# The first block of a two-layer attention and Mish kernel: order of loads, folds and products, and the order of its first stage

## The chip, the cores and the metric

The kernel runs on one core of one Trainium2 chip. Its time is in device microseconds (us) for one execution. A profiled execution has a span, from its first to its last instruction, and a time of its own a little above it. Engines are named as in the profile: PE is TensorE's matmuls and PEld its weight loads, DVE is VectorE, ACT is ScalarE, POOL is GpSimd, and SP is SyncE, which here issues the loads and stores.

## The reference, cut to what matters

Two layers, each of two residual steps, on x of 2048 x 640 in float32:

```python
x = x + A(layernorm(x))      # 32 heads of 20
x = x + B(layernorm(x))      # 640 -> 1536 -> 640, Mish between
# A:
q, k, v = split(x @ wqkv)
pq, pk = q @ w_phi, k @ w_phi                       # per head, 20 x 20
phi = concat(softmax(p), softmax(-p))               # for pq and pk
kv, z = phi_k^T v, sum(phi_k)                       # over the 2048 rows
o = (phi_q kv) / (phi_q z + 1e-6);   return o @ wo
```

q and k are used only through `w_phi`, so the kernel multiplies `w_phi` into the query and key weights once, at the start of layer 0. That is the "fold".

## The kernel before, in words

**Precision.** Every large product is made of three: each operand is split into a high part (rounded by a copy on ACT) and a low part (the rest, subtracted on DVE or POOL), and TensorE adds high x high, high x low and low x high. A projection of one tile of 128 rows onto 640 columns is `project` (L329): two halves of 320 columns, five chunks of 128 inputs each, three products, so 30 matmuls at L344.

**Stages.** Rows come in 8 blocks of two tiles of 128. The first stage of a layer is `attend_first` (L387): queries, keys and values of all tiles, their features, and the sums kv and z. The second is `attend_second`, then comes `dense`. A tile's queries and keys go through `features` (L355), a generator that stops after each step: the copy out of PSUM on ACT; minimum, maximum and differences on DVE (POOL takes one difference of a query); the exponential on ACT; sum and reciprocal on DVE and a product on POOL. Each step of the loop calls `advance` (L399), which moves every pending generator one stop further. A key tile ends in 22 matmuls that add to kv and z (L414, 11 calls); a query tile ends in a transposition on DVE (L423) and four stores. `order` (L464 to L470) says which of k, q and v of which tile comes at which of the six steps of a block. For a middle block it is k0, v0, q0, k1, v1, q1.

**PSUM and buffers.** PSUM has two wide tiles `mm` (L66), for projections, and four narrow ones `one` (L69); kv and z keep two of the narrow ones from block 0 to the end of the stage. Five `big` tiles hold key features and, at the end of the stage, reloaded query features.

**What orders the work.** The program text gives each instruction a place, and a planner (`tc.block(schedule_with_timeline_sim=True)`, L814) orders each engine from it by its own estimate of when operands are ready. `tc.manual_schedule(engines=...)` takes an engine's order from the text instead. `tc.issue_after(ins)` puts an instruction behind another one of the same engine, and `act` (L110) chains most of ACT's work that way. In the first block only SP is written by hand (L446).

**The first block of layer 0** (L445 to L458). SP loads, in this order: the first half of the table `phi_bd` of folded heads, chunks 0 to 2 of the transposed query weights (`load_raw`, 120 rows each), x of block 0 (`fetch_normed`, L390), the second half of the table, chunks 3 to 5. Then come five loads of value weights and six chunks of key weights. x is normalized: statistics on DVE (L250), a power on POOL (L260), two ACT operations (L303), then five transpositions of each tile on TensorE (L280) with their splits (L285, L286). `fold_phi` (L227) multiplies the chunks by the table: for each of five output rows k and two halves c, three products at L237 (the last chunk has 40 rows), then the split at L242 and L243. A product at L237 is in full float32 and appears as two instructions. `load_v_weights` splits the value weights (L127, L128). Block 0 takes v0, q0, v1, k0, q1, k1, and the key fold, `fold_phi` again, is called before k0 (L480).

Of the kernel before, what the change touches and what calls it, by code (L numbers as in the profile page):

```python
# [1 line left out]

# [6 lines left out]
F32 = mybir.dt.float32  # L9
# [33 lines left out]
def kernel(  # L43
# [76 lines left out]
    def v_tile():  # L120
        return work.tile([P, VW], F32, tag="v", name="v", bufs=2)

    def split(hi, lo, src, stage):

        st = stage()[:, :D]
        nc.sync.dma_start(st, src)
        nc.scalar.activation(hi, st, AF.Copy)  # L127
        nc.vector.tensor_tensor(lo, st, hi.bitcast(F32), op=ALU.subtract)  # L128

    def r1_spare(tag):  # L130
# [36 lines left out]
    def load_v_weights():  # L167

        ws = [r1_pair(k) for k in range(KD)]
        for k in range(KD):  # L170
            split(ws[k][0][:, D:2 * D], ws[k][1][:, D:2 * D], wv[k * P:(k + 1) * P, :],
                  (row_tile, row_tile, v_tile, v_tile, big_tile)[k])
        return ws

    def load_q_weights():
# [48 lines left out]
            raw.append((r, rows))  # L224
        return raw

    def fold_phi(ws, bd, raw):  # L227

        pss = {}
        for k, c in ((0, 0), (1, 0), (2, 0), (3, 0), (0, 1), (1, 1), (2, 1), (3, 1), (4, 0), (4, 1)):  # L230
            if c == 0:
                mm = None if k % 2 else mm_tile()
                pss[k] = [one_tile(), one_tile()] if k % 2 else [mm[:, 0], mm[:, 1]]
            ps = pss[k][c]
            for t in range(3 * c, 3 * c + 3):
                r, rows = raw[t]
                nc.tensor.matmul(ps[:, (t % 3) * 120:(t % 3) * 120 + rows],  # L237
                                 r[:rows, k * P:(k + 1) * P], bd[:rows, t, :rows],
                                 start=True, stop=True)
            n0, n1 = (0, 360) if c == 0 else (360, D)  # L240
            hi, lo = ws[k][0][:, n0:n1], ws[k][1][:, n0:n1]
            nc.scalar.activation(hi, ps[:, :n1 - n0], AF.Copy)  # L242
            nc.vector.tensor_tensor(lo, ps[:, :n1 - n0], hi.bitcast(F32), op=ALU.subtract)  # L243


    def norm_stats(t, xt):
# [79 lines left out]
        return Transposed(cols=cols)  # L326


    def project(xts, t, ws, col, ps=None):  # L329
# [57 lines left out]
    def attend_first(layer, x_src, first):  # L387


        def fetch_normed(b):  # L390
            if layer:
                return load_turned(n2_d[b], [row_tile] * 3)
            xt = fetch(x_src, b)
# [12 lines left out]
        def keys(xts, i, v):  # L406
            e = big_tile()
            yield from features(project(xts, i % BT, kv_ws, 0), e, False)
            yield
            for g in range(G):  # L410
                p, n = divmod(g, 2)
                w, m = (120, 64) if g < 10 else (80, 42)
                acc, c = (kva, 120 * p) if p < 4 else (kvz, 120 * (p - 4))
                nc.tensor.matmul(acc[64 * n:64 * n + m, c:c + w], v[:, GW * g:GW * g + m],  # L414
                                 e[:, 120 * g:120 * g + w],
                                 start=(i == 0 and p in (0, 4)), stop=(i == NT - 1),
                                 skip_group_check=True)
# [12 lines left out]

        def values(xts, i, v):
            vv = v.rearrange("p (h d) -> p h d", d=DH + 1)
            act(vv[:, :, DH], ident[:, :H], AF.Copy, scale=0.0, bias=1.0)
            if i < BT:
                pv = project(xts, i, kv_ws, D, [one_tile(), one_tile()])
# [7 lines left out]
            yield  # L443

        if first is None:  # L445
# [12 lines left out]
            nc.sync.dma_start(mask, head_mask)  # L458
        else:
            nxt, kv_ws = first  # L460
            q_ws = load_q_weights()
        for b in range(NB):
            xts = nxt
            order = ("k0", "v0", "q0", "k1", "v1", "q1")  # L464
            if b == 0:
                order = ("v0", "q0", "v1", "k0", "q1", "k1")
            elif b == 1:
                order = ("k0", "q0", "k1", "v0", "q1", "v1")
            elif b == NB - 1:
                order = ("k0", "k1", "v0", "v1", "q0")  # L470
            vs = [v_tile() for _ in range(BT)]
            for n, (kind, t) in enumerate(order):
                t = int(t)
                i = b * BT + t
                if b == 0 and n == 1:
                    if layer:
                        load_k_weights(kv_ws)
                if b == 0 and n == 3:
                    if layer == 0:
                        fold_phi(kv_ws, bd, raw)  # L480
                    kva, kvz = one_tile(), one_tile()
                if b == NB - 1 and n == 3:
                    loaded = {0: load(0)}
                if b + 1 < NB:
                    if n == 0:
                        xt = fetch_normed(b + 1)
                    elif n == 2:
                        nxt = xt if layer else normed(b + 1, xt)
                    elif n > 2:
                        nxt.step()  # L490
                g = {"k": lambda: keys(xts, i, vs[t]), "q": lambda: queries(xts, i),
                     "v": lambda: values(xts, i, vs[t])}[kind]()
                next(g)
                advance()
                pending.append(g)
# [401 lines left out]
```

## Time and profile before

| | us |
|---|---|
| median of three runs | 1401.89 |
| lowest and highest | 1401.17, 1402.03 |
| the profiled execution | 1400.33 |
| its span | 1398.6 |
| TensorE busy (99%) | 1384.2 |
| VectorE busy (77%) | 1074.5 |
| ScalarE busy (42%) | 584.1 |
| GpSimd busy (32%) | 442.3 |

A line of the profile that names a group has the line of the program, the engine, the operation, the tiles (out<-in), shapes and count; then busy time and the mean length of one in ns; then the idle time of the engine just before these instructions and what ended it. A line in the order of time begins with its start and its length in us, and merges equal neighbours (x8). A line of stretches has the stretch, its length, the busy time and count of each engine, the granted clock of TensorE, the share of the DMA engines and GB/s. Matmuls overlap: one's length is its time in flight, and the distance between two starts is what it costs TensorE. So TensorE counts as busy also where it runs at half its pace.

### The profile page before, as it was taken

Reading aid. Unit: us, or ns where it says so; the run is one execution under the profiler, and the core shown is the slowest. Engines: PE = TensorE matmul, PEld = TensorE weight load, DVE = VectorE, ACT = ScalarE, POOL = GpSimd, SP = SyncE. Lnnn points to the kernel's source line nnn. Section 1 sums busy time; section 2 is a strip of 40 time slices with the busy share of each in tenths; the row PEclk is TensorE's granted clock in tenths of the full one; section 3 lists DMA queues with packets and bytes.
Section 4 is the critical chain, followed back from the end, with each engine's and each line's share of the span. In section 5 each row is a group of like instructions: output and inputs, shape, how many; then the busy total and the mean of one; then the engine's idle time right before and its main releaser. Section 6 shows DMA issues by size and latency. Waiting matters only on the chain. (4 is left out here: it accounts for less than half of the span.)

```text
span 1398.6 us, 28120 instructions
## 1 busy us (share of the span) xinstructions
PE 1384.2 (99%) x11528; PEld 1367.6 (98%) x11528; DVE 1074.5 (77%) x1820; ACT 584.1 (42%) x973; POOL 442.3 (32%) x334
## 2 busy tenths in 40 slices
PE   7999999999999999999999999999999999999998
PEld 7999999999999999999999999999999999999998
DVE  5798877696698877788769887887767876767775
ACT  4444344321355454545454333332234444444443
POOL 1354444343422222222234443433352211211112
PEclk9999999999999999999999999999999999999999
DMA  8533422689733423343374333357976212333200
GB/s 319 169 79 57 75 40 39 185 237 292 254 87 95 111 75 64 91 114 95 106 273 89 71 65 69 50 109 218 288 251 208 69 26 77 95 95 95 73 24 20
DMA packets 350035, 169.57 MB, mean 121 GB/s; under 512 B 286866, under 2 KB 323458, under 8 KB 349906
## 3 DMA queue, kind: packets, MB, share of 16 engines
q1 hardware_dynamic: 349906, 167.78, 44.2%
q8 instruction: 90, 1.47, 0.4%
q14 instruction: 39, 0.32, 0.1%
HBM read 104.82 MB, written 62.91 MB: 120 GB/s over the span
## 5 line engine op out<-in xcount | busy, mean ns | idle before, releaser
L735 PE MATMUL mm<-r2h,ol 128*128 128x320 f32 x1280 | 304.7, 309 | 0.0
L719 POOL TENSOR_TENSOR ol<-big,ol 128x512 fp32r<-128x512 f32 (+1 forms) x98 | 129.8, 1325 | 484.1 <-ACT ol L718 407.8
L693 PE MATMUL one<-xtl,r1h 128*128 128x256 f32 x960 | 268.2, 279 | 0.0
L693 PE MATMUL one<-xth,r1l 128*128 128x256 f32 x960 | 268.0, 279 | 0.0
L693 PE MATMUL one<-xth,r1h 128*128 128x256 f32 x960 | 265.9, 279 | 0.0
L735 PEld LDWEIGHTS mm<-r2h,ol 128*128 128x128 f32 x1280 | 219.1, 188 | 0.0
L735 PE MATMUL mm<-r2l,ol 128*128 128x320 f32 x640 | 197.3, 309 | 0.0
L344 PE MATMUL mm<-r1h,xth 128*128 128x320 f32 x600 | 188.3, 314 | 0.0
L344 PE MATMUL mm<-r1h,xtl 128*128 128x320 f32 x600 | 185.7, 310 | 0.7 <-DVE xtl L286 0.7
L344 PE MATMUL mm<-r1l,xth 128*128 128x320 f32 x600 | 185.6, 309 | 0.0
L693 PEld LDWEIGHTS one<-xtl,r1h 128*128 128x128 f32 x960 | 180.4, 188 | 0.0
L693 PEld LDWEIGHTS one<-xth,r1l 128*128 128x128 f32 x960 | 180.4, 188 | 0.0
L693 PEld LDWEIGHTS one<-xth,r1h 128*128 128x128 f32 x960 | 179.6, 188 | 0.0
L708 DVE TENSOR_SCALAR big<-big 128x512 f32<-128x512 f32 (+1 forms) x98 | 56.4, 575 | 110.7 <-ACT big L706 110.5
L379 POOL TENSOR_TENSOR r<-r,r 128x1280 f32<-128x1280 f32 x32 | 75.8, 2367 | 142.6 <-DVE r L378 136.8
L735 PEld LDWEIGHTS mm<-r2l,ol 128*128 128x128 f32 x640 | 120.2, 188 | 0.0
L710 ACT ACTIVATE big<-big,two 128x512 f32<-128x512 f32 (+1 forms) x98 | 70.1, 715 | 116.1 <-DVE big L709 116.1
L706 ACT ACTIVATE big<-one,b1s 128x256 f32<-128x256 f32 x192 | 80.8, 467 | 90.2 <-PE one L693 89.7
L718 ACT ACTIVATE ol<-big 128x512 fp32r<-128x512 f32 (+1 forms) x98 | 61.0, 622 | 135.8 <-DVE big L717 135.7
L344 PEld LDWEIGHTS mm<-r1h,xth 128*128 128x128 f32 x600 | 112.8, 188 | 2.0
L344 PEld LDWEIGHTS mm<-r1h,xtl 128*128 128x128 f32 x600 | 112.8, 188 | 1.1 <-DVE xtl L286 1.0
L344 PEld LDWEIGHTS mm<-r1l,xth 128*128 128x128 f32 x600 | 112.8, 188 | 0.0
(129 smaller groups left out, 3158.1 us busy)
## 6 DMA issues: line engine op xcount, KB each, us to landing
e_d<-r SPq DMA_DIRECT2D x128, 160.0 KB, 4.0
big<-e_d SPq DMA_DIRECT2D x32, 640.0 KB, 6.8
x_d<-xt SPq DMA_DIRECT2D x23, 640.0 KB, 4.1
xt<-x_d SPq DMA_DIRECT2D x22, 640.0 KB, 4.4
n_d<-xn SPq DMA_DIRECT2D x176, 80.0 KB, 2.1
xt<-in_x SPq DMA_DIRECT2D x16, 640.0 KB, 5.7
xn<-x_d SPq DMA_DIRECT2D x28, 320.0 KB, 4.6
v<-n_d SPq DMA_DIRECT2D x30, 256.0 KB, 2.9
```

The costliest lines, as they stand in the source:

```text
L344: nc.tensor.matmul(ps[:, :HC], a[:, sl], r, start=(k == 0 and n == 0), stop=(k == KD - 1 and n == 2))
L379: nc.gpsimd.tensor_tensor(eg, eg, r.unsqueeze(2).to_broadcast([P, 2 * H, DH]), op=ALU.mult)
L693: nc.tensor.matmul(ph[:, j, :], l, r, start=(n == 0), stop=(n == 3 * KD - 1))
L706: exps[0] = nc.scalar.activation(part(ta, 0)[:, j - js.start], ph[:, j, :], AF.Exp, bias=b1s[:, 2 * pr + j:2 * pr + j + 1]).ins
L708: nc.vector.tensor_scalar_min(e, e, E_CAP)
L710: nc.scalar.activation(r, n, AF.Ln, bias=two)
L718: nc.scalar.activation(ah[:, js], n, AF.Copy)
L719: nc.gpsimd.tensor_tensor(al[:, js], n, ah[:, js].bitcast(F32), op=ALU.subtract)
L735: nc.tensor.matmul(pys[t][:, c, :HC], l[:, j, sl], r, start=(f == 0 and n == 0), stop=(f == KF - 1 and n == 2))
```

## The change

1. **Warm transposes.** Before everything else TensorE transposes the identity 36 times into a narrow PSUM tile that nobody reads (`keep_warm`), and four times more between each two of the first three fold chunks.
2. **Loads.** x of block 0 is loaded first. The loads of x of block 1 and of the mask are issued behind the key chunks.
3. **Written order.** In the first block, and through all six steps of block 0 of layer 0, TensorE follows the text.
4. **Query fold by chunk.** The first halves of all five rows are folded chunk by chunk (five rows with chunk 0, then chunk 1, then 2), and split; then come the transposes of x; then the second halves, one piece between each two groups of three products of the first half of q0.
5. **Order of block 0.** q0 comes first: q0, v0, v1, k0, q1, k1. The value weights are split on ACT behind the last query piece. The ten key pieces stand one by one between the ten groups of three products of v1.
6. **By kinds.** Middle blocks (2 to 6, in both layers) take k0, k1, v0, v1, q0, q1, and a key of an even tile of blocks 2 to 6 gets one more stop ahead of its accumulation, which so comes in the same step as that of the odd tile.

The diff, cut to its core:

```diff
+    warm = one_tile()
+    def keep_warm(n):
+        for _ in range(n):
+            nc.tensor.transpose(warm[:, :P], ident, ident)
+    keep_warm(36)
...
-    def split(hi, lo, src, stage):
+    def split(hi, lo, src, stage, behind):
...
-        nc.scalar.activation(hi, st, AF.Copy)
+        with nullcontext() if behind is None else tc.issue_after(behind):
+            nc.scalar.activation(hi, st, AF.Copy)
...
+    def fold_heads(bd, raw, k, t, ps):
+        r, rows = raw[t]
+        nc.tensor.matmul(ps[:, (t % 3) * 120:(t % 3) * 120 + rows], r[:rows, k * P:(k + 1) * P],
+                         bd[:rows, t, :rows], start=True, stop=True)
+    def fold_split(ws, k, c, ps):
+        n0, n1 = (0, 360) if c == 0 else (360, D)
+        hi, lo = ws[k][0][:, n0:n1], ws[k][1][:, n0:n1]
+        ins = nc.scalar.activation(hi, ps[:, :n1 - n0], AF.Copy)
+        nc.vector.tensor_tensor(lo, ps[:, :n1 - n0], hi.bitcast(F32), op=ALU.subtract)
+        return ins.ins
+    def fold_part(ws, bd, raw, k, c, ps):
+        for t in range(3 * c, 3 * c + 3):
+            fold_heads(bd, raw, k, t, ps)
+        return fold_split(ws, k, c, ps)
...
         for c in range(2):
-            project_half(ps[c], xts, t, ws, col, c)
+            for ks in [range(KD)] if between is None else [range(k, k + 1) for k in range(KD)]:
+                project_half(ps[c], xts, t, ws, col, c, ks)
+                if between is not None:
+                    next(between, None)
...
             yield from features(project(xts, i % BT, kv_ws, 0), e, False)
             yield
+            if i % BT == 0 and BT < i < NT - BT:
+                yield
...
-            with tc.manual_schedule(engines={mybir.EngineType.SP}):
+            with tc.manual_schedule(engines={mybir.EngineType.PE, mybir.EngineType.SP}):
+                xt = fetch_normed(0)
                 bd = big_tile()[:120, :720].rearrange("p (t c) -> p t c", t=6)
                 nc.sync.dma_start(bd[:, :3], phi_bd[:, :3])
                 raw = load_raw(0, range(3))
-                xt = fetch_normed(0)
                 nc.sync.dma_start(bd[:, 3:], phi_bd[:, 3:])
                 raw += load_raw(0, range(3, 6))
-                nxt = normed(0, xt).all()
+                nxt = normed(0, xt)
                 q_ws = [r2_pair(k) for k in range(KD)]
-                fold_phi(q_ws, bd, raw)
-                kv_ws = load_v_weights()
+                ps = [h for mm in (mm_tile(), mm_tile()) for h in (mm[:, 0], mm[:, 1])] + [one_tile()]
+                for t in range(3):
+                    for k in range(KD):
+                        fold_heads(bd, raw, k, t, ps[k])
+                    keep_warm(4 if t < 2 else 0)
+                for k in range(KD):
+                    fold_split(q_ws, k, 0, ps[k])
+                nxt.all()
+                mm = mm_tile()
+                q0 = [mm[:, 0], mm[:, 1], mm]
+                project_half(q0[0], nxt, 0, q_ws, 0, 0, range(1))
+                for k in range(KD):
+                    folded = fold_part(q_ws, bd, raw, k, 1, one_tile())
+                    project_half(q0[0], nxt, 0, q_ws, 0, 0, range(k + 1, min(k + 2, KD)))
+                project_half(q0[1], nxt, 0, q_ws, 0, 1)
+                kv_ws = load_v_weights(folded)
                 raw = load_raw(1)
-            nc.sync.dma_start(mask, head_mask)
+                xt = fetch(x_src, 1)
+                nc.sync.dma_start(mask, head_mask)
+            def fold_keys():
+                for k in range(KD):
+                    mm = mm_tile()
+                    for c in range(2):
+                        fold_part(kv_ws, bd, raw, k, c, mm[:, c])
+                        yield
...
-            order = ("k0", "v0", "q0", "k1", "v1", "q1")
+            order = ("k0", "k1", "v0", "v1", "q0", "q1")
             if b == 0:
-                order = ("v0", "q0", "v1", "k0", "q1", "k1")
+                order = ("v0", "q0", "v1", "k0", "q1", "k1") if layer else ("q0", "v0", "v1", "k0", "q1", "k1")
...
+            with written(b == 0 and not layer):
...
-                    if layer == 0:
-                        fold_phi(kv_ws, bd, raw)
```

`written(on)` is `tc.manual_schedule` of TensorE, or nothing. `queries` of tile 0 gets the finished q0, and `values` of tile 1 gets `fold_keys()` as `between`.

More of the change, by code (lines that the diff above doesn't have):

```diff
@@ L1 @@
-from contextlib import ExitStack
+from contextlib import ExitStack, nullcontext
 import concourse.bass as bass
@@ L165, in r2_pair, with load_v_weights @@
         return tuple(wts.tile([P, D], F32R, tag=f"r2{s}{j}", name=f"r2{s}{j}") for s in "hl")
-    def load_v_weights():
+    def load_v_weights(behind=None):
         ws = [r1_pair(k) for k in range(KD)]
@@ L171, in load_v_weights @@
             split(ws[k][0][:, D:2 * D], ws[k][1][:, D:2 * D], wv[k * P:(k + 1) * P, :],
-                  (row_tile, row_tile, v_tile, v_tile, big_tile)[k])
+                  (row_tile, row_tile, v_tile, v_tile, big_tile)[k], behind)
         return ws
@@ L225, in load_raw @@
         return raw
[L227 to L243, printed above, removed]
+    def fold_heads(bd, raw, k, t, ps):
[12 more added lines that the diff above has]
+        return fold_split(ws, k, c, ps)
     def norm_stats(t, xt):
@@ L326, in load_turned, with project @@
         return Transposed(cols=cols)
-    def project(xts, t, ws, col, ps=None):
+    def project(xts, t, ws, col, ps=None, between=None):
         if ps is None:
@@ L387, in attend_first, with fetch_normed @@
     def attend_first(layer, x_src, first):
-        def fetch_normed(b):
+        def fetch_normed(b, xt=None):
             if layer:
                 return load_turned(n2_d[b], [row_tile] * 3)
-            xt = fetch(x_src, b)
+            xt = fetch(x_src, b) if xt is None else xt
             norm_scale(b, [norm_stats(t, xt) for t in range(BT)])
@@ L429, in queries, with values @@
                     yield
-        def values(xts, i, v):
+        def values(xts, i, v, between=None):
             vv = v.rearrange("p (h d) -> p h d", d=DH + 1)
@@ L434, in values @@
             if i < BT:
-                pv = project(xts, i, kv_ws, D, [one_tile(), one_tile()])
+                pv = project(xts, i, kv_ws, D, [one_tile(), one_tile()], between)
                 for c in range(2):
@@ L471, in attend_first @@
             vs = [v_tile() for _ in range(BT)]
[L472 to L478, printed above, removed]
-                    if layer == 0:
-                        fold_phi(kv_ws, bd, raw)
[L481 to L495, printed above, removed]
+            with written(b == 0 and not layer):
+                for n, (kind, t) in enumerate(order):
+                    t = int(t)
+                    i = b * BT + t
+                    if b == 0 and n == 1:
+                        if layer:
+                            load_k_weights(kv_ws)
+                    if b == 0 and n == 3:
+                        kva, kvz = one_tile(), one_tile()
+                    if b == NB - 1 and n == 3:
+                        loaded = {0: load(0)}
+                    if b + 1 < NB:
+                        if n == 0:
+                            xt = fetch_normed(b + 1, xt if b == 0 and not layer else None)
+                        elif n == 2:
+                            nxt = xt if layer else normed(b + 1, xt)
+                        elif n > 2:
+                            nxt.step()
+                    g = {"k": lambda: keys(xts, i, vs[t]), "q": lambda: queries(xts, i, q0 if first is None and i == 0 else None),
+                         "v": lambda: values(xts, i, vs[t], fold_keys() if first is None and i == 1 else None)}[kind]()
+                    next(g)
+                    advance()
+                    pending.append(g)
             if b == 1:
```

2 lines of the change are left out of this document (added).

## The prediction

> **What bounds the kernel now.** I read the page first, then the waits of TensorE, then the order of time around the first block and around one middle block, and last a few stretches.
>
> ```profile
> span 1398.6 us, 28120 instructions
> PE 1384.2 (99%) x11528; PEld 1367.6 (98%) x11528; DVE 1074.5 (77%) x1820; ACT 584.1 (42%) x973; POOL 442.3 (32%) x334
> PE   7999999999999999999999999999999999999998
> ```
>
> TensorE is full in every slice of 35 us but the first (and the tail of the last). So the change can win in the first 35 us, or by making TensorE's own work shorter. The waits of TensorE (who waited for what: us in total, times, longest) agree: the first fold (L237) waits 7.9 us for three loads, and the next entry is 0.9.
>
> ```profile
> PE mm L237 <- DMA raw<-in_wqk_t: 7.9, 3, 4.2
> PE mm L571 <- PE mm L571: 0.9, 2, 0.4
> ```
>
> A second loss hides inside "busy". In the order of time (start, length, engine, line, tiles, count):
>
> ```profile
> 0.99 0.29 POOL masks.py:199 TENSOR_SCALAR_AFFINE_SELECT ident<-ident 128x128 f32<-128x128 f32 x1
> 4.18 1.18 PE L237 MATMUL mm<-big,raw 120*128 120x120 f32 x4 [4.18 <-DMA raw<-in_wqk_t]
> ...
> 11.14 2.10 PE L237 MATMUL mm<-big,raw 120*128 120x120 f32 x8 [2.22 <-DMA raw<-in_wqk_t]
> 13.17 1.07 PE L237 MATMUL mm<-big,r 40*128 40x40 f32 x4
> 14.23 0.90 PE L280 MATMUL one<-ident,xn 128*128 128x128 f32 x3
> 14.93 1.48 PE L237 MATMUL one<-big,raw 120*128 120x120 f32 x6
> 16.20 1.70 PE L280 MATMUL one<-ident,xn 128*128 128x128 f32 x7
> 17.69 1.09 PE L237 MATMUL mm<-big,raw 120*128 120x120 f32 x6
> ...
> 45.61 0.60 PE L237 MATMUL mm<-big,raw 120*128 120x120 f32 x4
> 46.14 0.41 PE L237 MATMUL mm<-big,r 40*128 40x40 f32 x2
> 46.48 0.41 PE L344 MATMUL mm<-r1l,xth 128*128 128x320 f32 x1
> ```
>
> From 16.20 to 17.69 seven transposes start 0.213 us apart, and the six fold products before them 0.212. At 45.61 four fold products fit in 0.60 us; less one product's 0.27 in flight that is 0.11 apart. So TensorE is half as fast at first and doubles within the row of 17.69 (six products in 1.09), at about 18.3. It had worked without a pause since 11.14: that took 7.15 us.
>
> To compare the two kernels I take a point that both reach. The last fold piece of before ends at 46.48, and by then these instructions are done (stretch, its length, busy and count of TensorE, then of its weight loads; L237, L344 and L280 in turn):
>
> ```profile
> 0.00:46.47 46.47, 20.63 (x120) 18.83 (x120) 1.00 0.82 299
> 0.00:46.47 46.47, 16.40 (x103) 15.14 (x103) 1.00 0.82 299
> 0.00:46.47 46.47, 4.14 (x20) 3.07 (x20) 1.00 0.82 299
> ```
>
> All 120 fold instructions (a call at L237 is two of them), 103 projection matmuls, 20 transposes. I walk the changed block until TensorE has done as much.
>
> **The first block after the change.** Prices first: the splits on ACT and DVE (of fold pieces, of transposes, of value weights: count, busy, mean ns), two places where TensorE goes from folds to projections, and the way of x to its normalized rows.
>
> ```profile
> L242 ACT ACTIVATE r2h<-mm 128x360 fp32r<-128x360 f32 x3 | 1.4, 473 | 6.5 <-PE mm L237 6.5
> L116 ACT ACTIVATE xth<-one 128x512 fp32r<-128x512 f32 x3 | 1.8, 594 | 0.2 <-PE one L280 0.2
> L286 DVE TENSOR_TENSOR xtl<-one,xth 128x512 fp32r<-128x512 f32 x3 | 2.0, 683 | 0.2 <-ACT xth L116 0.2
> L127 ACT ACTIVATE r1h<-v 128x640 fp32r<-128x640 f32 x2 | 1.5, 737 | 0.0
> L128 DVE TENSOR_TENSOR r1l<-v,r1h 128x640 fp32r<-128x640 f32 x2 | 1.6, 814 | 0.0
> 25.80 0.42 PE L344 MATMUL one<-r1h,xth 128*128 128x320 f32 x1
> 26.05 0.31 PE L344 MATMUL one<-r1l,xth 128*128 128x320 f32 x1
> 43.02 0.83 PE L237 MATMUL mm<-big,raw 120*128 120x120 f32 x6
> 43.61 0.39 PE L344 MATMUL mm<-r1h,xth 128*128 128x320 f32 x1
> 9.92 1.66 DVE L250 BATCH_NORM_STATS2 bn<-xt 128x6 f32<-128x320 f32 x4
> 13.26 0.92 ACT L113 ACTIVATE xn<-xt,stats 128x640 f32<-128x640 f32 x1 [3.83 <-DVE stats L262]
> 15.00:20.00 5.00, 5.00 (x32) 5.00 (x31) 5.00 (x14) 5.00 (x11) 2.00 (x3) 1.00 1.04 401
> 803.21 13.40 PE mm L344 x90
> ```
>
> A second-half fold piece (4 + 2 instructions) takes 46.48 - 45.61 = 0.87; a first-half one (6) takes 43.61 - 43.02 = 0.59 behind transposes, and I take 0.65 between projections. The first projection matmul behind a piece holds TensorE 0.25 (25.80 to 26.05); in a long run one takes 13.40 / 90 = 0.149. So a group of three behind a piece takes 0.55.
>
> 1. Warm transposes. They need only the identity, ready at 0.99 + 0.29 = 1.28, so they start at 1.4. By the one example here TensorE doubles 7.15 later, at 8.55: 34 at 0.213, two at 0.11, end 8.85.
> 2. First halves of the query fold, chunk by chunk: 30 x 0.11 and twice four warm transposes, 8 x 0.11, together 4.2: end 13.05. Loads don't hold this: half table, three chunks and x are the first five loads in both kernels, and x, their last before, was in by 9.92. Now x is first; its way to two normalized rows (13.26 + 2 x 0.92 - 9.92 = 5.2) from about 5 on is over by 10.2, hidden. Ten transposes: 14.15.
> 3. The chunk order finishes five pieces nearly at once, so on ACT their high halves queue ahead of those of the transposes: first piece at 12.4, 5 x 0.47 = 14.75, then 0.59 and DVE's 0.68: 16.05. This wait is new; the first three products end at 16.2, 1.5 late.
> 4. Five second-half pieces (4.35) with four groups of three between (2.2), then 15 products (2.3): query tile 0 is done at 25.1.
> 5. Value weights are split behind the last query piece on ACT, from 23.2: 0.73, then on DVE 5 x 0.81, end 28.0. TensorE needs the last part at about 26.9, so value tile 0's first half ends at 28.15, the second 15 x 0.149 later: 30.4. Late by 1.1.
> 6. Value tile 1 with ten key pieces: 10 x 0.55 + 5 x 0.87 + 5 x 0.65 = 13.1, end 43.5. The switches (0.10 for each group behind a piece) are 1.0 of this and 0.5 of step 4. ACT and DVE need about half a us for a piece against 1.3 on TensorE, which hides them.
> 7. To the same point: 13 projections and ten transposes of the next block, 3.1. End **46.6**, against 46.48.
>
> So the front is worth **+0.1**: what it gains by starting early and without load waits is paid back by 8.85 us before the first useful product, 0.9 of inner warm transposes, 2.6 of waits for ACT and DVE, 1.5 of switches. Bounds: -1.7 to +3.1 by the moment of doubling, and up to +2.7 by DVE's order (rivals).
>
> Written order means that all of TensorE queues behind a late operand; steps 3 and 5 are such places. On the load queue mask, x of block 1 and the key chunks now come behind five value loads. The key chunks are needed first at about 31; the queue moves 401 GB/s (stretch from 15 to 20), 0.8 for a load of 327,680 bytes, and has them in by 21. I cost that at nothing; if the cover failed, each load late is 0.8.
>
> **The order by kinds.** In blocks 2 to 6 of both layers two keys come first, and the extra yield puts the even tile's accumulation (L414) beside the odd one's. Groups of 22 and of 44 and what follows them:
>
> ```profile
> 118.90 1.38 PE L414 MATMUL one<-big,v 128*64 128x120 f32 x22
> 120.21 0.42 PE L344 MATMUL mm<-r1h,xth 128*128 128x320 f32 x1
> 267.98 2.54 PE L414 MATMUL one<-big,v 128*64 128x120 f32 x44
> 270.45 0.41 PE L344 MATMUL one<-r2h,xth 128*128 128x320 f32 x1
> ```
>
> 22 take 1.31 and 44 take 2.47, so a merged pair saves 0.15, and up to 0.10 more where one slow re-entry into projections goes: I take 0.19, near the first. Ten blocks: **-1.9**. Bounds: 0 if they don't merge, -2.5 with all of it.
>
> **Sum.** 0.1 - 1.9 = -1.8. The profiled execution took 1400.33 (span 1398.6 and 1.7 around it), 1.56 under the median of the runs, 1401.89. The difference goes onto the median: **1400.1 us**.
>
> **Rivals.**
>
> (a) TensorE doubles sooner. The 7.15 us contain 1.06 of 40-row products (13.17 to 14.23) that may not count like full ones. If it doubles at 5.0, 17 transposes at 0.213 and 19 at 0.11 end at 7.1. The first chunk ends 1.16 MB of loads; 0.5 MB were in at 4.18 and 1.81 MB at 9.92, so about 7.1 too. Steps 2 to 7 come 1.75 earlier: 1398.4. [...]
>
> (b) Transposes alone don't raise the speed. Then 36 slow ones end at 9.07, the doubling comes 7.15 after the first product, at 16.2, and step 2 ends at 16.7, not 13.05. ACT keeps up with slow products, which gives back 0.6: +3.1, **1403.2**. For it: no row shows a doubling on transposes alone. Against it: from 14.23 to 17.69 transposes took 2.19 of 3.46, and the doubling came next. [...]
>
> (c) DVE is held by x of block 1. That load lies behind 20 others, 6.8 MB with its own: 1.81 by 9.92, then 0.4 a us, so about 22.5. If its statistics (1.66 and some 0.3) stand in DVE's order ahead of the second-half low parts, these end at 26.7 and the value parts at 30.7, not 28.0: +2.7, 1402.8. It decides only if the planner puts them there.
>
> (d) Slower. Keys and queries of neighbouring blocks now come four in a row, and DVE falls behind. Stretches of one middle block and of the last one (length, busy of PE, PEld, DVE, ACT, POOL):
>
> ```profile
> 118.90:149.37 30.47, 30.47 (x236) 29.85 (x235) 25.25 (x35) 12.16 (x17) 13.87 (x9) 1.00 0.37 66
> 240.00:268.00 28.00, 28.00 (x217) 27.19 (x215) 21.31 (x24) 9.18 (x12) 13.09 (x7) 1.00 0.56 118
> ```
>
> A block asks 25.25 of DVE in 30.47. Should all of it fall in four of six steps (20.3), DVE lags 4.9; without statistics and transposes (1.9 and 3 x 0.6), 1.2. ACT's next copy stands behind an exponential that waits for DVE, and with two PSUM tiles TensorE is held from a lag of one projection on, 30 x 0.149 = 4.5. At a lag of 5.2 each of ten blocks loses 0.7: +7, **1407**. Against it: the last block already runs keys, keys, values, values, query with TensorE full.
>
> (e) The change doesn't do all it says: from block 1 on the planner, not the text, orders TensorE. Groups kept apart cost the 1.9: 1402.0. It belongs to the forecast's own spread.
>
> **How the numbers follow.** Forecast with (e) 0.38 (own range 1398.3 to 1402.0), (a) 0.24, (b) 0.14, (c) 0.10, (d) 0.14. The range leaves out (d) and a little at both ends: **1396.5 to 1404.5**. A measurement of this kernel can tell about 0.2%, 2.8 us: faster is under 1399.1, slower over 1404.7. Faster: 0.18 of (a), 0.14 of the forecast, 0.02 of others, 0.34. Slower: 0.13 of (d), 0.04 of (b) and (c), 0.17. Same: 0.49.
>
> **What will show it.** Transposes from 1.4 on, 0.213 apart and then 0.11: where that changes decides between forecast, (a) and (b). TensorE waiting at 14 to 16 for the halves of the transposes, and in value tile 0 for L128's parts. Groups of 44 at L414 in blocks 2 to 6 in 2.47, no new wait at L344 or L414. The forecast is wrong if the work counted above (120, 103, 20) is done far from 46.6, or if what follows it is shorter by other than 1.9.

## The result and the profile after

The changed kernel takes 1410.25 us (median of 6 runs, 1408.29 to 1413.59), the kernel before 1401.53 in the same session (1400.68 to 1402.90): a ratio of 1.0065, interval 1.0053 to 1.0077. It is slower by 0.65%, and its time lies outside the range of the prediction. The profiled execution took 1408.29, the fastest of the six; its span is 1406.5. Lines below are those of the changed kernel (in the runs whose edits add lines, the same groups stand up to two lines further on); fold products are now L239, their splits L245 (ACT) and L246 (DVE), projections L356, transposes L289, warm transposes L92, key accumulation L428, value splits L136 (ACT) and L137 (DVE), statistics L259.

The page first, which hardly tells the two apart:

```profile
span 1406.5 us, 28222 instructions
PE 1387.9 (99%) x11572; PEld 1370.8 (97%) x11572; DVE 1073.5 (76%) x1820; ACT 584.6 (42%) x973; POOL 440.5 (31%) x334
PE   8899999999999999999999999999999999999998
```

TensorE is "busy" 3.7 us more for 44 more instructions, and the second slice of 35 us now shows an 8. The waits of TensorE say where (who waited for what: us in total, times, longest):

```profile
PE mm L239 <- DVE r1l L246: 6.2, 5, 2.3
PE mm L356 <- DVE r2l L246: 1.7, 1, 1.7
...
PE mm L356 <- DMA v<-in_wv: 1.3, 1, 1.3
PE one L356 <- DVE r1l L137: 1.0, 2, 0.8
```

The load waits of before are gone; five waits of fold products for DVE stand in their place. In the order of time (start, length, engine, line, tiles, count, idle time before it and what ended that):

```profile
1.34 5.55 PE L92 MATMUL one<-ident 128*128 128x128 f32 x36 [1.34 <-POOL ident masks.py:199]
6.89 1.12 PE L239 MATMUL mm<-big,raw 120*128 120x120 f32 x8
...
11.17 1.26 PE L289 MATMUL one<-ident,xn 128*128 128x128 f32 x10
13.72 0.42 PE L356 MATMUL mm<-r2h,xth 128*128 128x320 f32 x1 [1.29 <-DMA v<-in_wv]
...
24.84 0.41 PE L356 MATMUL mm<-r2l,xth 128*128 128x320 f32 x1 [1.70 <-DVE r2l L246]
...
32.49 0.82 PE L239 MATMUL mm<-big,raw 120*128 120x120 f32 x6
...
36.02 0.70 PE L239 MATMUL mm<-big,raw 120*128 120x120 f32 x4 [2.26 <-DVE r1l L246]
...
41.03 0.70 PE L239 MATMUL mm<-big,raw 120*128 120x120 f32 x4 [2.21 <-DVE r1l L246]
...
49.20 0.70 PE L239 MATMUL mm<-big,raw 120*128 120x120 f32 x4 [0.68 <-DVE r1l L246]
```

The start is better than forecast. The chunk products begin at 6.89 (8.85 was forecast), and the last query piece ends 1.9 us earlier than in the forecast's steps, at 20.82. From there on it is lost. Query tile 0's second half and value tile 0 end at 32.05, 11.23 us for a forecast of 7.65, and value tile 1 with the ten key pieces runs to 53.65, 21.60 us for a forecast of 13.1. Two stretches of that time, the second from the first key piece on (length, busy of PE, PEld, DVE, ACT and POOL, granted clock, DMA):

```profile
22.80:32.49 9.69, 6.77 (x38) 5.19 (x37) 9.69 (x23) 3.32 (x7) 3.74 (x4) 1.00 0.90 359
32.49:53.65 21.16, 14.97 (x89) 12.72 (x87) 7.32 (x21) 8.42 (x17) 4.22 (x7) 0.92 0.42 156
```

In the first DVE is the full engine, 9.69 of 9.69. In the second no engine is full, and TensorE idles 6.2: engines that wait for each other in turn. The granted clock is under 1 there; stretches of 2 us show that it is halved for 3.4 us, from 41.8 to 45.2:

```profile
40.00:42.00 2.00, 0.96 (x6) 0.85 (x6) 1.10 (x5) 0.00 (x0) 0.93 (x3) 0.95 0.42 164
42.00:44.00 2.00, 2.00 (x10) 1.92 (x10) 0.68 (x3) 0.84 (x2) 0.15 (x1) 0.50 0.27 102
44.00:46.00 2.00, 1.65 (x8) 1.28 (x8) 0.53 (x1) 0.47 (x1) 0.00 (x0) 0.70 0.60 234
```

The work that before had done by 46.5 us (120 fold products, 123 projections and transposes of rows) is done at 56.8: +10.3. (The mix differs a little: 109 projections and 14 transposes, before 103 and 20.) At the end of the span +7.9 is left, so what follows the front is 2.4 shorter. The merged accumulation is there, 44 in a row; it starts 8.63 after the group of 267.98 in before:

```profile
276.61 2.54 PE L428 MATMUL one<-big,v 128*64 128x120 f32 x44
279.08 0.41 PE L356 MATMUL one<-r2h,xth 128*128 128x320 f32 x1
```

### The profile page after: what moved, and what is told of

It reads as the page before. It is cut to its first block, busy times and chain, and to the rows that moved or that the text cites. A ratio compares the mean times of both kernels' runs of the same rounds, so it can differ in the third digit from the quotient of the medians.

```text
span 1406.5 us, 28222 instructions
## 1 busy us (share of the span) xinstructions
PE 1387.9 (99%) x11572; PEld 1370.8 (97%) x11572; DVE 1073.5 (76%) x1820; ACT 584.6 (42%) x973; POOL 440.5 (31%) x334
## 5 line engine op out<-in xcount | busy, mean ns | idle before, releaser
L356 PE MATMUL mm<-r1h,xth 128*128 128x320 f32 x600 | 187.6, 313 | 0.0
L356 PE MATMUL mm<-r1h,xtl 128*128 128x320 f32 x600 | 185.7, 310 | 0.7 <-DVE xtl L295 0.7
L356 PE MATMUL mm<-r1l,xth 128*128 128x320 f32 x600 | 185.8, 310 | 0.0
L356 PEld LDWEIGHTS mm<-r1h,xth 128*128 128x128 f32 x600 | 112.7, 188 | 1.4
L356 PEld LDWEIGHTS mm<-r1h,xtl 128*128 128x128 f32 x600 | 112.8, 188 | 1.2 <-DVE xtl L295 1.0
L356 PEld LDWEIGHTS mm<-r1l,xth 128*128 128x128 f32 x600 | 112.8, 188 | 0.0
```

The lines of the kernel that those rows point to most:

```text
L356: nc.tensor.matmul(ps[:, :HC], a[:, sl], r, start=(k == 0 and n == 0), stop=(k == KD - 1 and n == 2))
```

## The experiments

Two theories stood at the start. **Shared tile:** a key piece's second half waits because the first half of the same wide PSUM tile isn't split yet. **Statistics:** DVE stands at the statistics of x of block 1 until x lands, with low parts behind them that TensorE needs (rival (c) of the prediction). Their rival for the whole: the order by kinds stalls, and the front is a lesser matter.

| label | what | median us (lowest to highest) | ratio to before, interval |
|---|---|---|---|
| kinds_alone | before + order by kinds | 1398.10 (1396.28 to 1398.95) | 0.9977, 0.9968 to 0.9987 |
| block_alone | change without order by kinds | 1414.35 (1409.36 to 1415.88) | 1.0088, 1.0067 to 1.0108 |
| own_tiles | change, narrow tile for each key piece | 1399.97 (1398.88 to 1401.91) | 0.9991, 0.9982 to 1.0001 |
| x1_early | change, x of block 1 loaded sooner | 1418.04 (1413.32 to 1420.56) | 1.0116, 1.0094 to 1.0138 |
| stats_behind | own_tiles, statistics of block 1 later | 1399.28 (1395.56 to 1404.44) | 0.9983, 0.9970 to 0.9995 |
| split_free | stats_behind, value splits not held back | 1408.46 (1407.32 to 1409.02) | 1.0044, 1.0027 to 1.0061 |
| own_cold | own_tiles without warm transposes | 1400.53 (1399.28 to 1402.18) | 0.9991, 0.9982 to 1.0001 |
| kinds_warm | kinds_alone with 36 warm transposes | 1399.49 (1397.38 to 1400.68) | 0.9982, 0.9972 to 0.9991 |
| stats_12 | stats_behind, block 2's statistics later too | 1399.96 (1396.98 to 1402.22) | 0.9986, 0.9977 to 0.9995 |
| halves_apart | change, other order of key pieces | 1404.17 (1401.74 to 1406.15) | 1.0017, 1.0007 to 1.0027 |

**kinds_alone and block_alone: the change in two.** The kernel before with only this, and the changed kernel with only this undone:

```diff
-            order = ("k0", "v0", "q0", "k1", "v1", "q1")
+            order = ("k0", "k1", "v0", "v1", "q0", "q1")
...
+            if i % BT == 0 and BT < i < NT - BT:
+                yield
```

> Only the order by kinds, on the kernel before. Theory (the order by kinds gains, the first block loses): ten merged accumulations give 1.7 to 1.9 us, so 1399.7 and a span about 1.8 under the 1398.6 of before. Rival (four features in a row delay DVE and the middle blocks stall, as the slower rival of the prediction had it): 1404 or more, with new waits at L344 between 100 and 270 us.

> The whole change but the order by kinds (middle blocks as before). Theory: the first block alone costs 10 us, so 1411.5 to 1412, 1.8 above the changed kernel. Rival (the loss comes from the order by kinds): within 2 us of the 1401.5 of before.

The order by kinds alone gives 0.23%, 3.2 us, more than the 1.7 to 1.9 expected, and doesn't stall. In its span, 4.1 shorter, 1.06 is the first block, whose loads came in sooner in that execution (the last fold piece starts at 44.55, before at 45.61); the rest, 3.0, is 1.5 in each layer. The chain of before in the second layer shows where (start, us, what):

```profile
801.90 1.31 PE one L414 x22
803.21 13.40 PE mm L344 x90
```

The chain of kinds_alone there (one record of the 44 is missing):

```profile
803.93 2.47 PE one L416 x43
806.40 26.59 PE mm L344 x180
```

A merged pair saves 2 x 1.31 - 2.47 = 0.15 in the accumulation, and 2 x 13.40 - 26.59 = 0.21 in the projections around it. The forecast took 0.19 for both, near the first; the whole stretch of a layer shows 1.5 / 5 = 0.30 a pair. The first block alone costs 0.88%, so all of the loss is in it. Its 1414.35 is above the 1411.5 to 1412 expected; in its profiled execution the clock is halved twice, for 13.7 us each time (last section).

**own_tiles: the shared tile.**

```diff
-                    mm = mm_tile()
                     for c in range(2):
-                        fold_part(kv_ws, bd, raw, k, c, mm[:, c])
+                        fold_part(kv_ws, bd, raw, k, c, one_tile())
```

> The changed kernel, but each of the ten key pieces gets a narrow PSUM tile of its own instead of one half of a shared wide tile. Theory: a second-half piece waits for the split of the first half because both lie in one tile; those five waits are 6.2 us, and the halved clock from 41.9 to 45.5 goes with them: 7 us less, 1402 to 1403.5, the clock at 1.00 through 30 to 55. Rival (DVE and ACT are late by themselves, whatever tile the piece has): waits of the same length move to the next piece, 1408 or more.

Ten us come back in the medians, more than the 7 expected; between the two profiled executions it is 7.1. The stretch of value tile 1 and the key pieces in own_tiles (columns as above), and then its waits of TensorE in the first 62 us:

```profile
33.02:45.13 12.11, 12.11 (x89) 11.30 (x87) 6.50 (x20) 7.39 (x17) 3.40 (x7) 1.00 0.69 257
```

The waits:

```profile
PE mm L356 <- DVE r2l L246: 1.9, 2, 1.3
...
PE one L356 <- DVE r1l L137: 0.5, 2, 0.4
```

The same 89 instructions take 12.11 in place of 21.16, TensorE is full, and its clock is 1.00 (it was 0.50 shortly before, from 27.32 to 30.73). No wait of L239 is left. Of the 9.05, instruction starts give 7.84 to the product groups and 1.21 to the pieces. The five groups ahead of a second half, which contain the waits, have 7.4 of the first. The groups and pieces that ran between 41 and 46 at half pace are about 1.2 of both together. So some 7.8 go with the waits and 1.2 with the clock.

**halves_apart: the same wide tiles, another order.** This shows whether it is the sharing or the width of the tile.

```diff
-                for k in range(KD):
-                    mm = mm_tile()
+                for ks in ((0, 1), (2, 3), (4,)):
+                    mms = [mm_tile() for _ in ks]
                     for c in range(2):
-                        fold_part(kv_ws, bd, raw, k, c, mm[:, c])
-                        yield
+                        for k, mm in zip(ks, mms):
+                            fold_part(kv_ws, bd, raw, k, c, mm[:, c])
+                            yield
```

> The changed kernel with its wide PSUM tiles for the key pieces, in another order: first halves of two heads' chunks, then their second halves (0 and 1, 2 and 3, then 4), as the kernel before had them apart; nothing else differs. Theory (a second half waits until the split of the first half in the same wide tile is done, some 1.25 us behind its end when ACT and DVE are free): with another piece and product between them (1.4 us) most of these waits go; the last pair keeps 0.7, the first pair about 1.1, since ACT and DVE are held there; v1 and the key pieces take 14 to 16 us in place of 21.2 and the clock keeps up or nearly so: 1402.5 (1400.5 to 1404.5). Rival: the split is late by itself (ACT and DVE have too much there, or the PSUM tiles come free too late), and the order changes nothing: waits of 6 us on the DVE split stay, 1408 to 1411.

The stretch is as expected. The wide tiles stay; with another piece between their halves 6.2 us of waits become 2.0:

```profile
PE mm L239 <- DVE r1l L246: 2.0, 3, 1.2
```

The stretch takes 15.09, in the middle of the 14 to 16 expected; the time, 1404.17, is near the upper end of its range:

```profile
34.32:49.41 15.09, 13.10 (x89) 11.31 (x87) 7.01 (x21) 8.31 (x17) 4.23 (x7) 1.00 0.59 219
```

**x1_early: the load of x of block 1 sooner.** A miss.

```diff
                 raw += load_raw(0, range(3, 6))
+                x1 = fetch(x_src, 1)
...
-                xt = fetch(x_src, 1)
+                xt = x1
```

> The changed kernel, but x of block 1 is loaded right behind the query chunks, ahead of the value weights. Theory: x of block 1 no longer holds DVE until 22.8 ahead of the last query piece and of the value parts; value tile 0 ends some 3 us earlier, 1406 to 1407.5. Rival (the value parts are bound by ACT's and DVE's splits anyway): under 1 us.

It is eight us slower than the changed kernel. The planner moved the statistics of x ahead on DVE (it must have expected x sooner); there DVE stood 5.46 us (start, length, idle time before):

```profile
7.96 0.23 DVE L271 SCALAR_TENSOR_TENSOR stats<-mv,stats 128x1 f32<-128x1 f32 x2 [1.24 <-POOL stats L269]
13.64 1.67 DVE L259 BATCH_NORM_STATS2 bn<-xt 128x6 f32<-128x320 f32 x4 [5.46 <-DMA xt<-in_x]
...
15.34 0.92 DVE L246 TENSOR_TENSOR r2l<-mm,r2h 128x360 fp32r<-128x360 f32 x2
```

Now all first-half low parts of the queries stand behind x, and the first products with them (4.8 us); the granted clock is 0.50 in every row from 20 to 30 and from 45 to 60. My theory named the right wait but the wrong remedy: the place in DVE's order has to change, not the load.

**stats_behind, split_free, stats_12: the place in DVE's order.** All three have narrow tiles. `lows` collects the DVE instructions of the value splits (in stats_12 those of the fold too):

```diff
-            norm_scale(b, [norm_stats(t, xt) for t in range(BT)])
+            with tc.issue_after(lows[-1]) if lows and b == 1 else nullcontext():
+                mvs = [norm_stats(t, xt) for t in range(BT)]
+            norm_scale(b, mvs)
```

stats_12 has `layer == 0 and b in (1, 2)` in place of `b == 1`. split_free has, beside the edit of stats_behind:

```diff
-                kv_ws = load_v_weights(folded)
+                kv_ws = load_v_weights()
```

> The changed kernel with each key piece in a narrow PSUM tile of its own (as in own_tiles), and in addition the statistics of x of block 1 on DVE issued behind the last low part of the value weights. Theory: in own_tiles the second half of q0 and value tile 0 (48 groups) take 11.18 us where 48 times 0.15 would be 7.2, because DVE stands at the statistics until x lands (22.7) and the last query low part and the five value low parts come behind them; behind them instead, the low parts run from 22.4 to about 26.6 and the pause shrinks from 4.0 to about 0.7 us: span some 3.3 shorter than own_tiles, 1396.7 (1395.8 to 1397.8). Rival: the value parts are late by themselves, since their high parts start on ACT only behind the last query piece (22.25 to 25.48): then a pause of 2 us or more stays and the time is 1398 to 1399. Second rival: the statistics, now later, hold up the first key pieces' low parts on DVE and give it back: 1399 to 1400.

> As stats_behind, and besides the value weights' high parts no longer wait on ACT for the last query piece (they may fill the gaps of about 1.0 us between the query pieces' high parts from 16.7 on; wv is in by 12.5 to 15.8). Theory: nothing of the value parts is late then, the 48 groups take 7.2 to 7.5 us, 0.3 to 1 below stats_behind: 1396.0 (1395.0 to 1397.0). Rival: the value parts of 0.73 (ACT) and 0.8 us (DVE) come ahead of query parts and TensorE waits for those, up to 0.6 us a piece: 1397 to 1399.

> As stats_behind (narrow tiles, block 1's statistics behind the value weights' low parts), and block 2's statistics on DVE behind the last low part of the key weights. Theory: stats_behind had the second half of q0 and value tile 0 in 8.03 in place of 11.18 us but met the same trouble once more: DVE stood 3.04 us at x of block 2 (landed about 41) with two key low parts behind it, TensorE paused 1.4 us, and its clock fell to 0.73 in 45 to 50, 1.55 us. Without both, the first key sums (73.93 in stats_behind, 72.78 in own_tiles, 71.43 in kinds_alone) start at about 70.8, and the time is 2 us below own_tiles: 1397.7 (1396.5 to 1399), about that of kinds_alone. Rival: the pause of 1.45 us ahead of the first products, which is in all of these, sets when the clock falls, and the spread of stats_behind (1395.6 to 1404.4) stays: median 1399 to 1400.

DVE in own_tiles, in the order of time:

```profile
22.71 1.67 DVE L259 BATCH_NORM_STATS2 bn<-xt 128x6 f32<-128x320 f32 x4 [1.29 <-DMA xt<-in_x]
24.30 0.43 DVE L246 TENSOR_TENSOR r2l<-one,r2h 128x280 fp32r<-128x280 f32 x1
24.64 0.82 DVE L137 TENSOR_TENSOR r1l<-xn,r1h 128x640 fp32r<-128x640 f32 x1
...
28.52 0.80 DVE L137 TENSOR_TENSOR r1l<-big,r1h 128x640 fp32r<-128x640 f32 x1
```

DVE in stats_behind, with a row of later on:

```profile
22.34 0.45 DVE L248 TENSOR_TENSOR r2l<-one,r2h 128x280 fp32r<-128x280 f32 x1 [0.97 <-ACT r2h L247]
22.96 1.56 DVE L139 TENSOR_TENSOR r1l<-xn,r1h 128x640 fp32r<-128x640 f32 x2 [0.18 <-ACT r1h L138]
...
25.91 0.82 DVE L139 TENSOR_TENSOR r1l<-big,r1h 128x640 fp32r<-128x640 f32 x1
26.65 1.67 DVE L261 BATCH_NORM_STATS2 bn<-xt 128x6 f32<-128x320 f32 x4
...
41.11 1.28 DVE L261 BATCH_NORM_STATS2 bn<-xt 128x6 f32<-128x320 f32 x3 [3.04 <-DMA xt<-in_x]
```

The mechanism holds: the last query low part comes 2 us sooner, and the 48 projections ahead of the first key piece (45, and the first three of value tile 1) take 8.03 us in place of 11.18. About 0.6 of the difference is the fallen clock of own_tiles: there the part from 29.38 to the first key piece takes 3.64, the same part of the changed kernel, at full clock, 3.05. But the time doesn't follow (1399.28, expected 1396.7; it lies in the range of the second rival, whose statistics were those of block 1). The last row tells why: DVE stands at the statistics of the next block, 3.04 us, with key low parts behind them, TensorE pauses 1.4, and its clock is 0.73 in the stretch from 45 to 50. stats_12 removes that, too, and its first accumulation starts at 69.96 (own_tiles 72.78). The lead is given back in block 1. Two stretches of stats_12, and the row of ACT that TensorE waits for there:

```profile
60.00:80.00 20.00, 20.00 (x153) 19.69 (x152) 20.00 (x26) 11.23 (x15) 11.50 (x8) 1.00 0.21 59
80.00:100.00 20.00, 17.95 (x148) 16.89 (x149) 19.97 (x25) 4.93 (x8) 9.79 (x7) 1.00 0.45 69
88.55 0.70 ACT L124 ACTIVATE r<-mm 128x640 f32<-128x640 f32 x1 [9.83 <-DMA e_d<-r]
```

TensorE loses 2.05 there, and at the first group of 44 the lead is down to 0.5 (124.41 against 124.91). ACT's copy of a query stood 9.83 us until the store of an earlier query had freed the buffer. DVE, busy in all of the first stretch, transposed that query at 79.37, in own_tiles at 73.80. So 2.8 us in front became 0.5; that DVE's full queue is the reason is argued from these rows and not tested. The theory of stats_12 is wrong on the time. Its 1399.96 lies in the rival's range, but not for the rival's reason: in the profiled execution the clock is 1.00 in all rows from 10 to 55 and from 60 to 80. split_free's rival names the cause, which was far larger than stated (1408.46 for 1397 to 1399): on ACT the value splits went ahead of the query parts, and the first products waited 6.5 us. The `behind` of the change is what prevents that.

**own_cold and kinds_warm: the warm transposes.** In own_tiles:

```diff
-    keep_warm(36)
+    keep_warm(0)
...
-                    keep_warm(4 if t < 2 else 0)
+                    keep_warm(0)
```

In kinds_alone:

```diff
     make_identity(nc, ident)
+    warm = one_tile()
+    for _ in range(36):
+        nc.tensor.transpose(warm[:, :P], ident, ident)
```

> own_tiles without the warm transposes (none of the 36 ahead and none of the 8 between the chunks). Theory (clock window as the trace of after shows it, TensorE's pace doubles 3 to 4.3 us after it becomes busy): first chunk product at 7.3, doubling near 11, transposes end about 15.3 in place of 14.7: span 0.5 to 1.2 longer than own_tiles, 1400.0 to 1401.3. Rival (the clock reading of the prediction, doubling 7.15 us after the start): all 30 chunk products, the transposes and part of the first products at half pace, 2.5 to 3.5 us: 1402.3 to 1403.6. Third: the warm transposes, which end at 7.99 where the first chunk lands at 7.2, cost as much as they bring: 1399.5 to 1400.

> The kernel before with the order by kinds (kinds_alone) and 36 transposes of the identity ahead of its first product, nothing else. Theory: the products and transposes that ran at half pace until 16.9 run at full pace, but the second three chunks land at 10.3 and the normalized rows of block 0 only at 13.3 and 14.1 on ACT, so that only the work behind 14.1 gains: 1.0 us (0.3 to 1.6) below kinds_alone, 1397.1. Rival: TensorE idles some 2.5 us ahead of the second chunks and its pace is halved again, no gain: 1397.8 to 1398.4.

Without them own_cold measures the same ratio as own_tiles, 0.9991, so the warm transposes cost as much as they bring, the third possibility of the expectation. Its chunk products start at 7.14, when the first chunk is in, and run at half pace to 12.4, 5.2 us behind the first one's start. The trace of the changed kernel, from which the expectation took 3 to 4.3, has one doubling, 3.0 behind its first transpose. TensorE in own_cold, in the order of time:

```profile
7.14 2.04 PE L239 MATMUL mm<-big,raw 120*128 120x120 f32 x8 [7.14 <-DMA raw<-in_wqk_t]
...
11.53 1.45 PE L239 MATMUL mm<-big,raw 120*128 120x120 f32 x8
12.82 0.39 PE L239 MATMUL one<-big,raw 120*128 120x120 f32 x2
...
15.08 0.39 PE L356 MATMUL mm<-r2h,xth 128*128 128x320 f32 x1 [0.78 <-ACT r2h L245]
```

TensorE in kinds_warm:

```profile
8.00 1.50 PE L241 MATMUL mm<-big,raw 120*128 120x120 f32 x12
10.60 1.54 PE L241 MATMUL mm<-big,raw 120*128 120x120 f32 x8 [1.10 <-DMA raw<-in_wqk_t]
12.06 0.64 PE L241 MATMUL mm<-big,r 40*128 40x40 f32 x4
15.01 0.90 PE L284 MATMUL one<-ident,xn 128*128 128x128 f32 x3 [2.31 <-ACT xn L117]
```

The first product of own_cold starts 0.34 later than in own_tiles (14.74): the pause ahead of it shrinks by what the chunk products take longer. In kinds_warm the transposes stand in the way of products that could have started at 4.04, and the pace they bring is lost again in the pauses before 10.60 and 15.01 (granted clock 0.50 in the stretch from 15 to 20). Its median is 1.4 above kinds_alone and above both ranges of the expectation, but the intervals of the ratios overlap: no gain is shown, and no sure loss.

No version is shown to beat kinds_alone, which is faster than both kernels.

## Why the prediction was wrong

The step that failed is 6, "ACT and DVE need about half a us for a piece against 1.3 on TensorE, which hides them". A duration hides behind another only if nothing waits for its result. I compared throughputs, but the second half of a piece went into the other half of the PSUM tile that the split was still reading: matmul, ACT, DVE and matmul became a chain, and TensorE paid 0.68 in the undisturbed case (at 49.20 and 52.68), 2.2 where ACT or DVE had something else ahead. For the pause that ends at 36.02 it was ACT, with the normalization of block 1; for the one that ends at 41.03 it was DVE, which stood at the statistics of block 2:

```profile
32.58 1.72 ACT L124 ACTIVATE xn<-xt,stats 128x640 f32<-128x640 f32 x2
38.45 0.49 DVE L259 BATCH_NORM_STATS2 bn<-xt 128x6 f32<-128x320 f32 x1 [2.48 <-DMA xt<-in_x]
```

The kernel before wrote its pieces (0,0), (1,0), (2,0), (3,0), (0,1) and so on, so that halves of a tile were apart; only (4,0) and (4,1) were neighbours, and there the planner put thirteen projections between them (43.61 to 45.61). I didn't count that order as something that the change removes. Measured against the forecast, in the profiled execution:

- **Steps 1 to 4, query tile's first half: 1.9 early.** TensorE's pace doubled 3.0 us after the start, on transposes alone. That is rival (a), at 4.3 where it had 5.0, and rival (b) is refuted. No trace shows that 5.0, nor the 1.7 of the bounds that comes from it: the one doubling of before is at 18.25, and behind the warm transposes it came at 4.25 (the changed kernel), 5.37 (block_alone) and 6.84 (own_tiles). The moment is in part luck: in own_tiles the pace doubled at 6.8, and the same point was only 0.9 early. The wait of step 3 was sized well (1.45 for 1.5), but own_tiles, where the same pause has its row with DVE r2l L246, puts its end on a low part of the query fold, not on the transposes' halves: query tile 0 takes a wide PSUM tile that a fold piece had (this is argued from the rows, no run tests it). The load that the row of 13.72 names is not among that product's operands.
- **Step 5, value tile 0: 3.6 late.** This stretch took 11.23 for 7.65. It is rival (c), to which I gave 0.10 and 2.7 us: the planner did put the statistics there, though only the last of the five query parts stood behind them; x landed at 22.7 (22.5 was estimated), and stats_behind is 3.15 shorter than own_tiles here, 0.6 of it by the clock. The prediction had the mechanism and gave it too little weight.
- **Step 6: 8.5 late,** 21.60 for 13.1; own_tiles brings it to 12.55, so the sum without the chain was right to 0.6.
- **Step 7** is as forecast, 3.15 for 3.1. Together -1.9 + 3.6 + 8.5 = +10.2; with the forecast's own +0.1 this is the +10.3.
- **The order by kinds: 1.1 to 1.3 better.** Right in mechanism; a pair is worth 0.30 and not 0.19. Rivals (d) and (e) are refuted: no new wait in blocks 2 to 6, and all ten pairs merged. The 7 us of (d) also rested on a lag of 5.2, where its own paragraph works out 4.9.
- **What the sum had no term for** is a pace that falls again. It is about 1.2 us here, and it differs from run to run: the mean granted clock of the six runs goes from 0.999 in the fastest to 0.990 in the two slowest. That fits a spread of 5.3 us, against 2.2 for the kernel before.

Without the chain the front still costs and isn't worth the +0.1 of the forecast. own_tiles has done the counted work at 48.3, 1.8 later than before (0.9 early at the last query piece, 3.1 late in step 5, 0.6 early in step 6), and starts its fourth accumulation at 100.31, before at 98.70. At the first one only 0.3 of that is to be seen (72.78, before 72.49). This agrees with the medians, 1399.97 against the 1398.10 of kinds_alone.

## What to carry to other kernels

Before a split or a copy is called hidden, ask which buffer it reads and who writes that buffer next: two halves of one tile written one after the other make a chain of what were parallel engines, and the profile shows it as a stretch in which no engine is full (here 21.16 us with TensorE, the fullest, busy for 14.97; 12.11 with a tile for each piece). Where a program order is handwritten on one engine and planned on the others, look for planned work that stands at a load with operands of the written engine behind it; moving the load can move the plan, as in x1_early, where DVE then stood 5.46 us, so fix the place. A gain in front can be given back in a later stage where other engines are behind, so follow the lead to its end before it is counted (in stats_12, 2.8 us became 0.5).

## What the hardware showed

- **The pace falls after short pauses, and changes in steps.** Pauses of 2.26 and 2.21 us, five us apart, were followed by a granted clock of 0.50 from 41.8 to 45.2. In block_alone and halves_apart one pause of 1.3 us, ahead of the first products, came before the first fall (to 0.50 at 15.61 in block_alone; 0.55 in the row from 15 to 20 in halves_apart). Stretches of block_alone, cut where its clock changes:

```profile
5.37:15.61 10.24, 8.95 (x77) 8.55 (x76) 5.33 (x15) 5.05 (x11) 1.09 (x3) 1.00 1.03 370
15.61:29.27 13.66, 13.66 (x50) 12.50 (x51) 6.55 (x15) 5.10 (x10) 1.45 (x3) 0.50 1.03 399
29.27:39.51 10.24, 7.98 (x55) 7.48 (x54) 6.58 (x16) 4.85 (x10) 3.88 (x5) 1.00 0.38 142
39.51:53.16 13.65, 11.99 (x46) 10.21 (x44) 4.84 (x14) 2.67 (x6) 1.07 (x3) 0.50 0.38 145
```

  In the second of these TensorE is busy all the time, 13.66 of 13.66, and runs at half pace: 50 instructions, where the first has 77 in 8.95. The lengths are three and four steps of 3.41 us. In the changed kernel the fall at 41.80 lasts 3.41 and comes 37.55, eleven such steps, behind the doubling at 4.25. By their rows of 5 us the falls of the other traces last about 3.4 (own_tiles, stats_behind, own_cold), 6.8 (kinds_warm), 13.7 (halves_apart), 17.0 and 20.5 (x1_early) and 20.5 (split_free): one, two, four, five and six steps. Where the steps lie differs: the first change, the doubling, is at 4.25 in the changed kernel, at 5.37 in block_alone, at 6.84 in own_tiles. In the changed kernel's own profile no fall followed the same pause (1.29 us; the clock is 1.00 from 4.25 to 41.80); in own_tiles, where TensorE's waits from the first products to 62 us are 1.3, 0.6 and two of together 0.5, the clock fell only at 27.32. The place among the steps doesn't settle it alone: the pause lies within one step in block_alone (12.20 to 15.61), where the fall followed, and in the changed kernel (11.08 to 14.49), where none did. What decides it stays open. In x1_early and split_free the clock fell during longer pauses, of 4.8 and 6.5 us (0.64 and 0.60 in the row from 15 to 20).
- **Transposes alone raise the pace.** In nine runs that start with 36 of them, spacing went from 0.213 to 0.11 after 3.0 us (the changed kernel, where the 36 take 5.55) to 5.6 us (kinds_warm, 6.82), before the first product.
- **The granted clock doesn't show the slow start.** It is 1.00 in all rows of the first 10 us, where the spacing says half pace (0.213 between transposes up to 4.17 in the changed kernel). The traces' record of the clock begins with the doubling (4.25 in the changed kernel, 18.25 in the kernel before), so the 1.00 ahead of it is not a reading; only the falls that come later show.
